# Transposing transfers that do not wait for one another: a fused state-space and feed-forward kernel

## The chip, the cores and the metric

The kernel runs on one core of a Trainium2 chip. The metric is the device time of one execution in microseconds (us). Before the change three runs took 178.19, 178.19 and 178.47 us, a median of 178.19. The core has engines that run at the same time, each with its own queue of instructions in a fixed order: TensorE (PE: matmuls; PEld: its weight loads), VectorE (DVE), ScalarE (ACT), GpSimd (POOL), and SyncE (SP), which here only issues transfers. They wait for one another through semaphores.

## The reference

The input x has 2048 rows of 512. It is normalized row by row, and the normalized xn feeds two branches whose results are added to x:

```
xn  = layernorm(x)
# A: a diagonal complex recurrence over the rows
Lam_bar = exp(dt * Lam);  B_bar = ((Lam_bar - 1) / Lam)[:, None] * B
h_t = Lam_bar * h_(t-1) + B_bar @ xn_t             (512 complex states)
A   = 2 * Re(C @ h_t) + xn * Dskip
# B: a gated feed-forward layer of width 1376
B   = (silu(xn @ w_gate) * (xn @ w_up)) @ w_down
out = x + A + B
```

All inputs and the output are bfloat16.

## The kernel before

The 2048 rows are cut into 4 chunks of 512, and each chunk into 4 tiles of 128 rows. Per chunk c the steps are: statistics and normalization of the four tiles (`bnst`, `bnag`, `ve`, `rstd`, `xn`); a transposition of the normalized tiles into xnT[c], with the features on the partitions; the gate and up matmuls (line 760), whose results ScalarE takes out of the accumulator banks (`silu` in line 772, `uev` in line 830) and VectorE multiplies into hT (line 832); the input matmuls of the recurrence against BT (line 881), which ScalarE takes out into u_sb (`uev_b`, line 888); the recurrence on VectorE, made real by rotating with cosine and sine tables, scanning (line 921) and rotating back into hss; and at last one accumulation of both branches into the output rows (lines 964, 978, 981), to which VectorE adds the residual (line 986) and which SyncE stores.

Chunk 0 is transposed on TensorE. Chunks 1 to 3 are transposed by a transposing transfer each, `xTd1` to `xTd3` (line 603), from xn_sb into xnT; for chunk 2 the destination lies in scrC, over the buffer tz that the tables use while they are made (`tm`, `tt1s`, `tzs`, `sinT`, `tt1c`, `tzc`, `cosT`, lines 707 to 722, once for each of 4 blocks). Four more transposing transfers bring in the weights of the recurrence: BT real and imaginary (`ld_bre`, `ld_bim`, lines 443 and 444) and C real and imaginary (`ld_cre`, `ld_cim`, lines 450 and 451). C lies in half of hss until ScalarE and VectorE have made W of it (lines 728 to 735).

All of these and nearly all plain loads go through SyncE's queue, in the order of the code: the x tiles of chunk 0 and the gate and up weights; the rows of chunk 1 (`ld_x4`); ld_bre, ld_bim, xTd1; the rows of chunks 2 and 3 (`ld_x8`, `ld_x12`) and Dskip (`ld_dsk`); ld_cre, ld_cim, xTd2; the down weights (`ld_wd0`, `ld_wd1`); xTd3; and the stores of the output.

Every transfer is made by the helper `dma` (line 394). A transposing one is given a dependence on all transfers created before it (line 397), and a plain one on the last transposing one (line 402). So a transposing transfer is never in flight together with any other transfer of the queue, and SyncE, which works in order, stands still in between.

The order on the engines is fixed when the program is built. `_schedule` is a planner: it gives each task a cost in ns and a priority (the longest path of costs behind it), keeps TensorE's and SyncE's tasks in the order of the code (`_CHAIN`), and fills the queues of VectorE, ScalarE and GpSimd by playing the program through. Of the tasks that could start within 200 ns of the earliest, it takes the one with the highest priority. A transfer counts as landed after 300 ns, its bytes at 330 bytes per ns behind the transfers ahead of it, and 2000 ns; a transposing one holds SyncE for 1900 ns and counts 1.2 times its bytes and 140,000 more, 769,145 for each of the seven. `_plan` then turns dependences into semaphore waits and leaves out those that an earlier wait already implies. `_emit` writes the instructions. The numbers of the planner decide the order alone; what the chip does is in the profile.

The accumulator has 8 banks, used as 4 pairs in rotation (`next_pair`, line 372). A pair is written by 8 matmuls, taken out by ScalarE, and written again four units later, so TensorE waits when ScalarE is more than three units behind.

Of the kernel before, what the change touches and what calls it, by code (L numbers as in the profile page):

```python
# [249 lines left out]
def bass_parallel_sum__ssm_conv_s5__swiglu_ffn__prompt_kernel(  # L250
# [32 lines left out]
    with es:  # L283
# [106 lines left out]

        dma_tasks = []
        xp_state = [None]

        def dma(name, dst, src, writes, nbytes, reads=(), after=(), out_=False, eng="sp", xpose=False, prio=0.0, order=(), **kw):
            after = tuple(after)
            if xpose:
                after = after + tuple(dma_tasks)
                fn = lambda e, dst=dst, src=src: e.dma_start_transpose(out=dst, in_=src)
                est, nb = 1900.0, int(nbytes * 1.2) + 140000
            else:  # L400
                if xp_state[0] is not None:
                    after = after + (xp_state[0],)
                fn = lambda e, dst=dst, src=src: e.dma_start(dst, src, **kw)
                est, nb = 330.0 + nbytes / 900.0, nbytes
            t = g.add(eng, fn, reads=reads, writes=writes, name=name, dma=True, after=after, out=out_, est=est, nbytes=nb, prio=prio, order=order)
            dma_tasks.append(t)
            if xpose:
                xp_state[0] = t
            return t

        TILEB = 128 * D * 2
# [4 lines left out]
        def pload(name, slot, src, **kw):  # L416
            return dma(name, prow[slot:128:8, :], src.rearrange("(a q j) -> q a j", a=4, q=4), [("prow", slot)], 1024, reads=[("prow0",)], **kw)

        def x_load(a, **kw):
            return dma("ld_x%d" % a, x_sb[:, a:a + 1, :], x_v[:, a:a + 1, :], [("x", a)], TILEB, **kw)  # L420

        def wg_load(nm, k0, k1, **kw):
            return dma("ld_wg" + nm, wg[:, k0:k1, 0:FG], wg_v[:, k0:k1, 0:FG], [("wg", nm)], (k1 - k0) * 128 * FG * 2, **kw)
# [659 lines left out]
```

## Time and profile before

The profiled execution took 178.43 us; its span from the first to the last instruction is 176.6 us.

| | |
|---|---|
| median of the runs | 178.19 us |
| profiled execution | 178.43 us |
| its span | 176.6 us |
| TensorE busy | 173.2 us, 98% |
| VectorE busy | 162.4 us, 92% |
| ScalarE busy | 87.1 us, 49% |
| GpSimd busy | 11.0 us, 6% |
| transposing transfers | 7, each 4.1 to 5.1 us from issue to landing |

How it is read: the page gives the busy time of each engine, then the span in 40 equal slices with the busy share of each in tenths (and the clock that TensorE was granted). The chain of work that ended last is followed back from the last instruction, and a list of it in order of time shows which engine set the pace when. A timeline lists the instructions of one engine, equal neighbours merged: start, duration, engine, line, operation, tile written and tiles read, count, and in square brackets how long the engine had been idle before and for whom. For SyncE the duration is that of the issue, not of the transfer. A list of waits says who waited for whom: total, times, longest.

### The profile page before, as it was taken

To read this page: it belongs to the slowest core of one execution; us is meant where nothing else is said; L and a number is where in the kernel's file an instruction comes from. 1 tells how busy PE (TensorE), PEld (TensorE's weight loads), DVE (VectorE), ACT (ScalarE), POOL (GpSimd) and SP (SyncE) were. 2 spreads that over 40 slices of the span, in tenths; PEclk is the share of its full clock that TensorE was granted. 3 is DMA by queue.
4 is the path that set the end of the run, shared out by engine and by line. 5 is a ranking of instruction groups with operands and counts; after the bars stand their busy time and mean duration, and the time that the engine had idled before them with its cause. 6 is when DMAs were issued, how large, how long until landed. Compare 5 with 4: busy or idle time off the path is not lost.

```text
span 176.6 us, 2364 instructions
## 1 busy us (share of the span) xinstructions
PE 173.2 (98%) x909; PEld 82.5 (47%) x916; DVE 162.4 (92%) x282; ACT 87.1 (49%) x116; POOL 11.0 (6%) x22
## 2 busy tenths in 40 slices
PE   8999999999999999999999999999999999999995
PEld 2894444444444444444444444444444444444543
DVE  2974999799999999999999999999999999999953
ACT  4679989979999668240456564000265620000000
POOL 3040500046000000000000000000000000000000
PEclk9999999999999999999999999999999999999999
DMA  5892668865675200001100000001100000000132
GB/s 169 269 370 75 119 137 103 267 121 119 119 267 132 43 0 0 0 4 60 61 0 0 0 0 4 0 0 59 59 0 4 0 0 0 0 0 4 41 119 78
DMA packets 22966, 12.37 MB, mean 70 GB/s; under 512 B 15308, under 2 KB 22956, under 8 KB 22956
## 3 DMA queue, kind: packets, MB, share of 16 engines
q1 hardware_dynamic: 22652, 11.77, 25.5%
q10 hardware_dynamic: 304, 0.46, 0.8%
q8 instruction: 7, 0.11, 0.3%
q14 instruction: 3, 0.02, 0.0%
HBM read 6.46 MB, written 2.10 MB: 48 GB/s over the span
## 4 chain that ended last, share of the span: by engine, by line
PE 96%; DMA 1%; DVE 1%; issue 0%; ACT 0%
PE pb L760 36%; PE pb L964 19%; PE pb L881 16%; PE pb L981 16%; PE pb L804 4%; PE pb L978 2%; PE pb L843 2%; DMA x_sb<-in_A_x_dram 1%; PE pb L853 1%; PE pb L583 1%; DVE st L529 0%; DVE xn_sb L516 0%; ACT sd L523 0%; DVE x_sb L986 0%; PE pb L476 0%
## 5 line engine op out<-in xcount | busy, mean ns | idle before, releaser
L921 DVE TENSOR_TENSOR_SCAN rot<-sm,car,rot 128x512 bf16<-128x512 f32 x32 | 38.7, 1265 | 0.0
L772 ACT ACTIVATE sg<-pb 128x1024 bf16<-128x1024 f32 x20 | 20.2, 1025 | 32.0 <-PE pb L760 31.3
L964 PE MATMUL pb<-wd,hT 128*128 128x512 bf16 (+2 forms) x166 | 34.7, 366 | 0.3 <-issue 0.2
L981 PE MATMUL pb<-W,hss 128*128 128x512 bf16 (+2 forms) x133 | 29.8, 366 | 0.2
L760 PE MATMUL pb<-xnT,wu 128*128 128x512 bf16 x120 | 27.9, 379 | 0.0
L964 PEld LDWEIGHTS pb<-wd,hT 128*128 128x128 bf16 x170 | 16.1, 98 | 18.9 <-ACT scrC L728 0.4
L830 ACT ACTIVATE uf<-pb 128x1024 bf16<-128x1024 f32 x20 | 20.5, 1026 | 7.6 <-PE pb L760 7.2
L760 PE MATMUL pb<-xnT,wg 128*128 128x512 bf16 x92 | 21.8, 379 | 0.0
L881 PE MATMUL pb<-xnT,BT 128*128 128x512 bf16 x96 | 21.2, 379 | 0.0
L981 PEld LDWEIGHTS pb<-W,hss 128*128 128x128 bf16 x136 | 12.9, 97 | 14.9
L888 ACT ACTIVATE u_sb<-pb 128x1024 bf16<-128x1024 f32 x16 | 16.3, 1020 | 5.3 <-PE pb L881 5.2
L760 PEld LDWEIGHTS pb<-xnT,wu 128*128 128x128 bf16 x120 | 11.7, 98 | 14.2 <-issue 0.2
L881 PEld LDWEIGHTS pb<-xnT,BT 128*128 128x128 bf16 x96 | 9.3, 98 | 11.6 <-DMA BT<-in_A_B_im_dram 0.5
L986 DVE TENSOR_TENSOR x_sb<-pb,x_sb 128x512 bf16<-128x512 f32 (+2 forms) x17 | 10.9, 655 | 3.5 <-PE pb L981 3.2
L760 PEld LDWEIGHTS pb<-xnT,wg 128*128 128x128 bf16 x92 | 9.0, 98 | 10.6
L832 DVE TENSOR_TENSOR hT<-sg,uf 128x1024 bf16<-128x1024 bf16 x20 | 13.4, 680 | 0.5 <-ACT uf L830 0.5
L481 DVE BATCH_NORM_STATS2 st<-x_sb 128x6 f32<-128x512 bf16 x12 | 7.5, 681 | 3.3 <-DMA x_sb<-in_A_x_dram 3.3
L912 DVE TENSOR_TENSOR rot<-u_sb,cosT 128x2048 bf16<-128x2048 bf16 x8 | 9.7, 1218 | 0.0
L912 DVE TENSOR_TENSOR rot<-rot,sin 128x2048 bf16<-128x2048 bf16 x8 | 9.7, 1218 | 0.0
L912 DVE TENSOR_TENSOR rot<-u_sb,sin 128x2048 bf16<-128x2048 bf16 x8 | 9.7, 1217 | 0.0
L912 DVE TENSOR_TENSOR rot<-rot,cosT 128x2048 bf16<-128x2048 bf16 x8 | 9.7, 1210 | 0.0
L912 DVE TENSOR_TENSOR rot<-rot 128x2048 bf16<-128x2048 bf16 x8 | 9.6, 1216 | 0.0
(93 smaller groups left out, 180.1 us busy)
## 6 DMA issues: line engine op xcount, KB each, us to landing
out_dram<-x_sb SPq DMA_DIRECT2D x15, 128.0 KB, 1.7
x_sb<-in_A_x_dram SPq DMA_DIRECT2D x3, 512.0 KB, 4.4
wd<-in_B_w_down_dram SPq DMA_DIRECT2D x1, 1280.0 KB, 6.2
wu<-in_B_w_up_dram SPq DMA_DIRECT2D x1, 768.0 KB, 5.0
wu<-in_B_w_up_dram SPq DMA_DIRECT2D x1, 608.0 KB, 7.1
x_sb<-in_A_x_dram SPq DMA_DIRECT2D x4, 128.0 KB, 3.4
wg<-in_B_w_gate_dram SPq DMA_DIRECT2D x1, 480.0 KB, 5.9
wg<-in_B_w_gate_dram ACTq DMA_DIRECT2D x1, 448.0 KB, 3.8
```

Of the source, the lines that this page charges most:

```text
L481: return g.add("dve", lambda e, a=a: e.bn_stats(out=st[:, a % 8, :], in_=x_sb[:, a, :]), reads=[("x", a)], writes=[("st", a % 8), ("st0", ...
L760: inst = e.matmul(pbank[0:fs, bk, :].rearrange("p (j t) -> p j t", j=4), lhsT=w[:, kt, i * 128:i * 128 + fs], rhs=xnT[c][:, :, kt, :], sta ...
L772: g.add("act", lambda e: e.activation(out=sg[rows, sl, 0:n, :].rearrange("p a t -> p (a t)"), in_=pair_f32(rows, bk, 512 * n), func=AF.Sil ...
L830: g.add("act", lambda e: e.activation(out=uf[rows, ul, 0:n, :].rearrange("p a t -> p (a t)"), in_=pair_f32(rows, bk, 512 * n), func=AF.Ide ...
L832: g.add("dve", lambda e: e.tensor_tensor(out=hT[rows, hb, i0:i0 + n, :], in0=sg[rows, sl, 0:n, :], in1=uf[rows, ul, 0:n, :], op=ALU.mult), ...
L881: inst = e.matmul(pbank[:, bk, :].rearrange("p (j t) -> p j t", j=4), lhsT=BT[:, ri, kt, pt * 128:(pt + 1) * 128], rhs=xnT[c][:, :, kt, :] ...
L888: g.add("act", lambda e: e.activation(out=u_sb[:, us].rearrange("p r t -> p (r t)"), in_=pair_f32(slice(0, 128), b0), func=AF.Identity), r ...
L912: tt = lambda out, a, b, op, r, w, nm: g.add("dve", lambda e: e.tensor_tensor(out=out, in0=a, in1=b, op=op), reads=r, writes=w, name="%s_% ...
L921: g.add("dve", lambda e, A0=A0, A1=A1, k=k, ri=ri, pt=pt: e.tensor_tensor_scan(out=A1[:, k, ri, :], data0=rr[:, pt:pt + 1].to_broadcast([1 ...
L964: inst = e.matmul(pbank[:, bk, 0:nc_], lhsT=hT[0:fs, hb, i, lt * 128:(lt + 1) * 128], rhs=wd[0:fs, i, c0:c0 + nc_], start=(i == 0), stop=F ...
L981: inst = e.matmul(pbank[:, bk, 0:nc_], lhsT=hss[:, hb, pt, ri, lt * 128:(lt + 1) * 128], rhs=W12[:, ri, pt, c0:c0 + nc_], start=False, sto ...
L986: g.add("dve", lambda e, bk=bk, a=a, c0=c0, nc_=nc_: e.tensor_tensor(out=x_sb[:, a, c0:c0 + nc_], in0=pbank[:, bk, 0:nc_], in1=x_sb[:, a, ...
```

## The change

A transposing transfer is no longer given a dependence on the transposing transfers ahead of it, only on the plain ones. A new list keeps the transposing ones, so that they can be left out. Dependences through data stay (a transposition of xn_sb still waits for the normalized tiles, and one into scrC for the readers of tz). A plain transfer depends on the last transposing one as before. The seven transposing transfers form the groups {ld_bre, ld_bim, xTd1}, {ld_cre, ld_cim, xTd2} and {xTd3}; within a group none waits any more for the landing of another. The planner sees the new dependences too.

```diff
         dma_tasks = []
         xp_state = [None]
+        xp_tasks = []
 
         def dma(name, dst, src, writes, nbytes, reads=(), after=(), out_=False, eng="sp", xpose=False, prio=0.0, order=(), **kw):
             after = tuple(after)
             if xpose:
-                after = after + tuple(dma_tasks)
+                after = after + tuple(t for t in dma_tasks if t not in xp_tasks)
                 fn = lambda e, dst=dst, src=src: e.dma_start_transpose(out=dst, in_=src)
                 est, nb = 1900.0, int(nbytes * 1.2) + 140000
...
             dma_tasks.append(t)
             if xpose:
                 xp_state[0] = t
+                xp_tasks.append(t)
             return t
```

## The prediction

> **What bounds the kernel now.** I read the engine totals and slices first, then the chain in order of time, then SyncE's queue and its waits, and last VectorE and ScalarE between 29 and 43 us, where the change reaches them.
>
> Totals and slices of the page:
>
> ```profile
> PE 173.2 (98%) x909; PEld 82.5 (47%) x916; DVE 162.4 (92%) x282; ACT 87.1 (49%) x116; POOL 11.0 (6%) x22
> PE   8999999999999999999999999999999999999995
> PEclk9999999999999999999999999999999999999999
> ```
>
> TensorE is busy from the second slice to the last, at the full granted clock; VectorE is close behind. The chain in order of time (start, length):
>
> ```profile
> 24.06 0.86 PE pb L881 x4
> 24.93 0.01 issue
> 24.93 13.12 PE pb L881 x60
> 38.06 17.27 PE pb L760 x80
> ```
>
> From 4.96 us on the chain is TensorE alone up to 174.82, with no piece of another engine between. 80 matmuls in 17.27 us are 0.216 us each, and no longer stretch runs slower. The order of TensorE's matmuls is that of the code, so the end can come earlier only where TensorE stands still. The pieces called issue after 5.4 us sum to 0.52 us; most lie where one matmul record is missing from a row (x39 for 40, x7 for 8). The one piece that touches a transfer of this change is 0.01 us, at 24.93, for BT's imaginary half.
>
> SyncE's queue (start, duration of the issue), and two of its waits:
>
> ```profile
> 16.25 2.26 SPq L398 DMA_TRANSPOSE BT<-in_A_B_re_dram  x1
> 20.74 1.99 SPq L398 DMA_TRANSPOSE BT<-in_A_B_im_dram  x1
> 24.96 2.93 SPq L398 DMA_TRANSPOSE xnT<-xn_sb  x1
> 30.07 0.93 SPq L403 DMA_DIRECT2D x_sb<-in_A_x_dram  x2
> ...
> 35.28 1.85 SPq L398 DMA_TRANSPOSE hss<-in_A_C_re_dram  x1
> ```
> ```profile
> SPq L398 <- DMA BT<-in_A_B_re_dram: 2.2, 1, 2.2
> SPq L244 <- DMA BT<-in_A_B_im_dram: 2.2, 1, 2.2
> ```
>
> Each transposing transfer takes 1.7 to 2.9 us to issue, and the next waits 2.2 to 2.5 us more for the landing. Four such waits go: 2.2 + 2.2 here, 2.5 + 2.4 at the two halves of C (the second is issued at 39.68, xTd2 behind it at 43.89).
>
> VectorE and ScalarE around the statistics of chunk 2:
>
> ```profile
> 29.94 1.29 DVE L711 SCALAR_TENSOR_TENSOR scrC<-scrC 128x512 f32<-128x512 f32 x2
> 31.14 0.76 DVE L717 TENSOR_SCALAR scrC<-scrC 128x512 f32<-128x512 f32 x2
> 31.81 0.68 DVE L719 SCALAR_TENSOR_TENSOR scrC<-scrC 128x512 f32<-128x512 f32 x1
> 33.44 2.47 DVE L481 BATCH_NORM_STATS2 st<-x_sb 128x6 f32<-128x512 bf16 x4 [0.94 <-DMA x_sb<-in_A_x_dram]
> ...
> 36.11 0.66 DVE L719 SCALAR_TENSOR_TENSOR scrC<-scrC 128x512 f32<-128x512 f32 x1
> ```
> ```profile
> 36.80 0.72 ACT L721 ACTIVATE cosT<-scrC,halfpi 128x512 bf16<-128x512 f32 x1 [1.04 <-DVE scrC L719]
> ...
> 38.71 2.93 ACT L505 ACTIVATE xn_sb<-x_sb,nmr,rstd 128x512 bf16<-128x512 bf16 x4 [0.28 <-DVE nmr L502]
> 41.55 1.01 ACT L888 ACTIVATE u_sb<-pb 128x1024 bf16<-128x1024 f32 x1
> ```
>
> VectorE waited 0.94 us for the rows of chunk 2, and ScalarE ran the four normalizations of chunk 2 ahead of one eviction that TensorE needs. That is TensorE's thinnest margin here: the eviction at 41.55 ends at 42.56, and its pair of banks is wanted 24 matmuls after 38.06, at 43.24.
>
> **The first group: BT real, BT imaginary, xTd1, the rows of chunk 2.** The real half stays at 16.25, since it waits for the plain load of chunk 1. The imaginary half can be issued at 16.25 + 2.26 = 18.5 instead of 20.74 and lands about 2.2 us earlier. On the path that is worth the 0.01 us; TensorE's weight loads lose a wait of 0.5 us there, hidden under matmuls, so 0.01 to 0.5 bounds the gain and I take 0.01, the matmuls' own row. xTd1 cannot move as far as its two waits suggest: it needs the four normalized tiles, whose row ends at 22.91, so it goes from 24.96 to about 22.95, a gain of 2.0. TensorE wants it at 24.06 + 32 x 0.216 = 30.97 and had it at about 30.05, so this gains nothing on the path; the cover is the 32 matmuls of chunk 0. xTd1 took 5.1 us to land; the other two transfers of its kind took 4.2 and 4.3. I take 5.1, the same transfer at nearly the same place: landing at 28.1, with 27.2 as the other end. The rows of chunk 2 took 30.07 to 33.44 = 3.37 us until VectorE read them, so they arrive at L = 31.5 (ends 30.6 and 31.5).
>
> **The order that the planner writes.** The landing estimates are inputs of the order on VectorE and ScalarE. By the planner's own arithmetic for before (its numbers decide order only; no time is taken from them) the rows of chunk 2 land at 31.7. With the imaginary half issued at 15.7 and landing at 20.7, xTd1 waits for the tiles at 20.9 and lands at 25.5, and the rows at 29.5. VectorE is free there at 29.6, after tzs2; bnst8 has priority 144.8 against 143.5 for tzs3. So the four statistics should move ahead of tzs3, tt1c2, tt1c3 and tzc2. Nothing ahead of that point changes place: the priorities of chunk 1's statistics fall by some 9 us but stay the highest.
>
> Cost of that, with durations of the trace: tzs2 ends at 30.6, VectorE then waits until L = 31.5, 0.9 us against 0.94 before. Statistics to the next instruction are 33.44 to 36.11 = 2.67, so tzs3 starts at L + 2.67 and its reader on ScalarE, sinT3, at L + 3.39 (the same pair at 23.43 and 24.15 shows 0.72). Behind sinT3 in ScalarE's queue I work out this order: one eviction (uev_b1_1), cosT2, the four normalizations, cosT3, then uev_b1_2. With starts 0.54, 0.90, 0.61, 2.84 and 0.61 apart (24.15 to 24.69, 42.45 to 43.35, 32.73 to 33.34, 38.71 to 41.55, and 0.61 again) uev_b1_2 starts at L + 8.89 and ends 1.01 later, L + 9.90, and some 0.06 passes to TensorE: L + 9.96 = 41.46. TensorE wants those banks 16 matmuls after 38.06, at 41.51. The stall is max(0, L - 31.55), so zero at the value taken, with 0.05 in hand; at L = 30.6 there is 0.95. The eviction after it, uev_b1_3, ends about 0.9 later, 42.4, against 43.24. ScalarE's other work up to there has room.
>
> **The second group: C real, C imaginary, xTd2, xTd3.** C real starts where the plain loads have landed, 2 us earlier; C imaginary follows it without 2.5. xTd2 then waits no longer for C but for cosT3, which reads the buffer it overwrites: about L + 8.28 + 0.72 = 40.5, plus the queue, so 41 against 43.89. That stall moves rather than goes. Nothing was waiting: xTd2 landed at 48.1 and is read from 55.16; wd landed at 54.6 and is read at 67.69; xTd3 landed near 58.9 and is read near 64.8; C landed by 43.9 and ScalarE first reads it at 51.60, in an order set by priority. Bounds: no gain above 0, no loss while covers of 4 us and more stand. W and the last gate tile (hL) have the thinnest later cover: hL ends at 74.08 against 76.11, 2.0 us; VectorE's wait at L would have to grow by that.
>
> Waits added: a reader of both C halves waits on two semaphores in place of one, on ScalarE at 51 us, off the path. Instructions, bytes and matmuls are the same.
>
> [...] All seven transposes are rows of SPq. [...]
>
> **Sum.** 0.01 gained, 0.00 lost. The profiled execution took 178.43 us (span 176.6 and 1.83 around it), 0.24 above the median of 178.19; the sum gives 178.42 on its own scale and 178.2 on the median's.
>
> **Rivals.**
>
> Stall behind the new order (slower): L comes later than 31.55, because xTd1 or the rows land slower than before. For it: the margin worked out is 0.05 us. Against: 5.1 was already the slowest of three. The end is later by L - 31.55; from L = 31.92 it exceeds 0.2%. At 32.4 it is 179.0.
>
> The halves of BT share the engines and land together (slower): nothing shows two in flight. The real half has 24.06 - 20.74 = 3.3 us in hand, so this decides only if it lands after 24.06. If both came only when the second came before, at 24.85, TensorE would stand 0.8 us: 179.0. Against: the second is issued 2.3 us behind the first, which should be half through.
>
> A gain at BT's imaginary half (faster): in unprofiled runs that wait might be larger than 0.01. The most the rows allow is the 0.5 of the weight loads: 177.7.
>
> The change does not do what it says: the second issue stays blocked until the first has landed and its row becomes 4 us long. Then all is as before, 178.2.
>
> **How the numbers follow.** 0.2% is 0.36 us, about what this kernel's measurement can tell from no change. Likeliest, no stall: 0.66, 178.2. No effect in the queue: 0.05, 178.2. Stall behind the new order beyond 0.36 us: 0.15. Halves together: 0.06. Gain beyond 0.36 us: 0.08. So faster 0.08, same 0.71, slower 0.21. The range goes from 177.95, half the bound of 0.5 below, to 179.0, where both slower rivals have their worked-out values; about 1 in 10 is left out.
>
> **What would show it.** Right: in SyncE's queue the imaginary half at 18.5 and xTd1 near 23; the statistics of chunk 2 directly behind one L711; the four normalizations near 36.9, ahead of the last cosT; TensorE's chain unbroken past 41.5. Wrong: a TensorE gap at 41.5 ended by ScalarE's L888, or at 24.06 ended by BT's real half, or a gap later ended by VectorE. A gain above 0.4 us would mean that TensorE waits in unprofiled runs where this profile shows none.

## The result, and the profile after

The changed kernel takes 179.22 us (median of 22 runs), the kernel before took 178.44 in the runs beside it: a ratio of 1.0046, with an interval of 1.0032 to 1.0060. The change makes the kernel 0.46% slower. The forecast was 178.2 us, no change, with a range up to 179.0; the second likeliest case, a stall behind the new order, was given 0.15, and it is what happens, but more often and larger than it was priced. A quarter of a microsecond of the miss is scale: the forecast stood on three runs of before with a median of 178.19, and 22 runs have 178.44. A ratio with its interval is given as recorded; it is not the quotient of the two medians beside it, and differs from that by up to 0.11%.

The runs of the changed kernel spread from 178.27 to 180.33 us, those of before from 178.10 to 179.02. They fall into two groups: with the 12 further runs of e1, 9 of 34 lie at 178.20 to 178.78 and 25 at 179.11 to 180.33, and none lies between. The profiled execution of the changed kernel took 178.51 us, less than nearly all its runs; its profile shows the new order but not the typical loss. A later profiled execution of the same kernel (run e11) took 179.88 us. Both are shown. Line numbers after the change are 1 or 2 higher.

Totals and slices of the page of the changed kernel (178.51 us):

```profile
PE 173.6 (98%) x909; PEld 83.0 (47%) x916; DVE 162.9 (92%) x282; ACT 87.9 (50%) x116; POOL 11.3 (6%) x22
PE   8999999999999999999999999999999999999995
```

Its chain in order of time (start, length), without a break where the BT matmuls and the gate and up matmuls of chunk 1 are:

```profile
24.33 13.81 PE pb L883 x64
38.14 17.27 PE pb L762 x80
55.41 6.91 PE pb L883 x32
```

Its queue of SyncE (start, duration of the issue):

```profile
15.95 2.08 SPq L399 DMA_TRANSPOSE BT<-in_A_B_re_dram  x1
18.09 3.24 SPq L399 DMA_TRANSPOSE BT<-in_A_B_im_dram  x1
22.72 1.77 SPq L399 DMA_TRANSPOSE xnT<-xn_sb  x1
27.30 0.93 SPq L404 DMA_DIRECT2D x_sb<-in_A_x_dram  x2
...
32.59 1.85 SPq L399 DMA_TRANSPOSE hss<-in_A_C_re_dram  x1
34.48 2.83 SPq L399 DMA_TRANSPOSE hss<-in_A_C_im_dram  x1
39.86 1.70 SPq L399 DMA_TRANSPOSE scrC<-xn_sb  x1
```

The waits are gone: each second transfer is issued as soon as the first issue is over, xTd1 is issued when the normalized tiles are there, and what follows is 2 to 5 us earlier. VectorE and ScalarE of the same execution:

```profile
29.70 0.68 DVE L713 SCALAR_TENSOR_TENSOR scrC<-scrC 128x512 f32<-128x512 f32 x1
30.65 2.47 DVE L483 BATCH_NORM_STATS2 st<-x_sb 128x6 f32<-128x512 bf16 x4 [0.27 <-DMA x_sb<-in_A_x_dram]
33.04 0.36 DVE L487 BATCH_NORM_AGGREGATE mv<-st 128x2 f32<-128x6 f32 x4
33.32 0.66 DVE L713 SCALAR_TENSOR_TENSOR scrC<-scrC 128x512 f32<-128x512 f32 x1
```
```profile
35.65 0.71 ACT L723 ACTIVATE cosT<-scrC,halfpi 128x512 bf16<-128x512 f32 x1
36.26 2.92 ACT L507 ACTIVATE xn_sb<-x_sb,nmr,rstd 128x512 bf16<-128x512 bf16 x4
39.08 0.71 ACT L723 ACTIVATE cosT<-scrC,halfpi 128x512 bf16<-128x512 f32 x1
39.69 1.91 ACT L890 ACTIVATE u_sb<-pb 128x1024 bf16<-128x1024 f32 x2
```

The statistics of chunk 2 now stand between the two L713, and on ScalarE the four normalizations and the last cosT stand ahead of two evictions. Here the rows came at 30.65 and nothing was late. In the execution of 179.88 us they came at 32.89. Its queue of SyncE, its VectorE, its ScalarE and its TensorE:

```profile
23.27 1.76 SPq L399 DMA_TRANSPOSE xnT<-xn_sb  x1
29.29 0.93 SPq L404 DMA_DIRECT2D x_sb<-in_A_x_dram  x2
```
```profile
32.89 2.48 DVE L483 BATCH_NORM_STATS2 st<-x_sb 128x6 f32<-128x512 bf16 x4 [1.95 <-DMA x_sb<-in_A_x_dram]
```
```profile
38.30 2.92 ACT L507 ACTIVATE xn_sb<-x_sb,nmr,rstd 128x512 bf16<-128x512 bf16 x4
...
41.74 1.91 ACT L890 ACTIVATE u_sb<-pb 128x1024 bf16<-128x1024 f32 x2
```
```profile
39.70 1.89 PE L762 MATMUL pb<-xnT,wu 128*128 128x512 bf16 x8
42.80 1.90 PE L762 MATMUL pb<-xnT,wg 128*128 128x512 bf16 x8 [1.20 <-ACT u_sb L890]
```

xTd1 took 6.02 us from issue to landing instead of the 4.58 of the first profile, VectorE waited 1.95 us for the rows, the eviction began at 41.74, and TensorE stood still for 1.20 us. That time is never made up: in the chain of that execution TensorE is without a piece of another engine from 42.80 to 176.28 us, 2 us before the end.

### The profile page after: what moved, and what is told of

The parts are those of the page before. It is cut to its first block, busy times and chain, and to the rows that moved or that the text cites. A ratio compares the mean times of both kernels' runs of the same rounds, so it can differ in the third digit from the quotient of the medians.

```text
span 176.7 us, 2363 instructions
## 1 busy us (share of the span) xinstructions
PE 173.6 (98%) x909; PEld 83.0 (47%) x916; DVE 162.9 (92%) x282; ACT 87.9 (50%) x116; POOL 11.3 (6%) x22
## 4 chain that ended last, share of the span: by engine, by line
PE 98%; issue 0%; DVE 0%
PE pb L762 36%; PE pb L966 19%; PE pb L883 16%; PE pb L983 16%; PE pb L806 4%; PE pb L478 3%; PE pb L980 2%; PE pb L845 2%; PE pb L855 1%; PE pb L585 1%; DVE x_sb L988 0%
## 5 line engine op out<-in xcount | busy, mean ns | idle before, releaser
L890 ACT ACTIVATE u_sb<-pb 128x1024 bf16<-128x1024 f32 x16 | 16.2, 1020 | 5.6 <-PE pb L883 5.4
L762 PE MATMUL pb<-scrC,wu 128*128 128x512 bf16 x40 | 9.4, 379 | 0.0
```

The costliest lines, as they stand in the source:

```text
L762: inst = e.matmul(pbank[0:fs, bk, :].rearrange("p (j t) -> p j t", j=4), lhsT=w[:, kt, i * 128:i * 128 + fs], rhs=xnT[c][:, :, kt, :], sta ...
L890: g.add("act", lambda e: e.activation(out=u_sb[:, us].rearrange("p r t -> p (r t)"), in_=pair_f32(slice(0, 128), b0), func=AF.Identity), r ...
```

## The experiments

The change does two things at once: it changes the waits on the chip, and, through the planner, the order on VectorE and ScalarE. The experiments take them apart. The changed kernel again (e1), the order alone (e2), the waits alone (e3) and a partial version (e4) ran on one chip, beside 29 runs of before with a median of 178.68 us.

**e1: the changed kernel again.**

> The changed kernel once more, for another profiled execution: the one at hand took 178.51 us, faster than nearly all its other runs (median 179.22), so it may not show what makes the typical run slow. Every theory expects a ratio near 1.005. Stall behind the new order: where the profiled execution is a slow one, TensorE stands still at about 41.6 us for ScalarE's eviction, and VectorE has waited longer than 0.3 us for the rows of chunk 2. Transfers in flight together: a gap at 24 to 31 us, ended by BT or by xTd1. Slow start: TensorE reaches its full rate later than 4.2 us, and the whole loss lies before 13 us.

Measured: 179.23 us, as at first; the ratio is 1.0020 (1.0001 to 1.0039). The profiled execution took 179.74: VectorE began the statistics at 32.74, and TensorE has a gap of 1.03 us that ends at 42.65 with ScalarE's eviction (L890). There is no gap at 24 to 31 us.

**e2: the new order with the old waits.**

```diff
+                xp_before[name] = tuple(xp_tasks)
                 after = after + tuple(t for t in dma_tasks if t not in xp_tasks)
...
         streams = _schedule(g.tasks, engs)
+        for t in xp_tasks:
+            t.deps.update(xp_before[t.name])
```

> The planner sees the new dependences, so the order on VectorE, ScalarE and GpSimd is that of the changed kernel, but the waits between the transposing transfers are put back after planning. The rows of chunk 2 then reach VectorE at about 33.4 us as before the change. Stall behind the new order: a stall of 33.4 - 31.55 = 1.9 us at TensorE near 41.5, ratio 1.010. Transfers in flight together: no pair is in flight, so ratio 1.000. Slow start from GpSimd's changed first instructions: ratio 1.005.

Measured: 180.38 us, ratio 1.0094 (1.0075 to 1.0112). The order alone costs 1.7 us. TensorE of this kernel:

```profile
25.22 13.12 PE L885 MATMUL pb<-xnT,BT 128*128 128x512 bf16 x60 [0.30 <-DMA BT<-in_A_B_im_dram]
...
43.73 1.90 PE L764 MATMUL pb<-xnT,wg 128*128 128x512 bf16 x8 [1.94 <-ACT u_sb L892]
```

The gap of 1.94 is the one that the theory of the order expected at 1.9; that the size fits so well is in part luck, since the rows came at 33.83 and not at 33.4, and TensorE was itself 0.46 us late by BT's imaginary half. No two transposing transfers were in flight together here, so that cannot be the cause.

**e3: the new waits with the old order.**

```diff
-                after = after + tuple(t for t in dma_tasks if t not in xp_tasks)
+                after = after + tuple(dma_tasks)
...
         streams = _schedule(g.tasks, engs)
+        for t in xp_tasks:
+            t.deps.difference_update(xp_tasks)
```

> The planner sees the old dependences, so the order on every engine is that of before, and the waits between the transposing transfers are taken out after planning. Stall behind the new order: nothing is late, ratio 1.000 (0.998 to 1.002). Transfers in flight together: ratio 1.005 as in the changed kernel, with a gap at 24 to 31 us. Slow start: 1.000.

Measured: 178.29 us, ratio 0.9976 (0.9961 to 0.9990): faster than before, where the theory of the order expected no change. Taking the waits out is a small gain; planning with them out is the loss.

**e4: only the BT group freed.**

```diff
-                after = after + tuple(t for t in dma_tasks if t not in xp_tasks)
+                after = after + tuple(t for t in dma_tasks if t not in xp_tasks or name not in ("ld_bre", "ld_bim", "xTd1"))
```

> Only the group BT real, BT imaginary, xTd1 is freed; C real, C imaginary and xTd2 wait as before. The order on VectorE and ScalarE is that of the changed kernel, GpSimd's first instructions are in the order of before. Stall behind the new order: ratio 1.005, as the changed kernel. Transfers in flight together at BT: 1.005; if the C group does the harm, 1.000. Slow start from GpSimd's order: 1.000.

Measured: 179.13 us, ratio 1.0019 (1.0005 to 1.0032), the same as the changed kernel beside it. The order on VectorE and ScalarE is the same too; the C group is not needed for the loss, and GpSimd's first instructions, which are back in the old order here, are not its cause. In the profiled execution, of 178.51 us, the rows came at 30.89 and there is no gap.

**e5 and e6: which wait is the gain.** Beside 29 runs of before with a median of 178.62 us. In e5, a version of the kernel before, the order stays and one wait goes:

```diff
         streams = _schedule(g.tasks, engs)
+        xp = {t.name: t for t in g.tasks if t.name in ("ld_bre", "ld_bim")}
+        xp["ld_bim"].deps.discard(xp["ld_bre"])
+        [t for t in g.tasks if t.name == "xTd1"][0].deps.add(xp["ld_bre"])
```

> Order on every engine as before; only the wait of BT's imaginary half for the landing of the real half is taken out (xTd1 still waits for both, the C group as before). If the gain of the waits alone (ratio 0.9976) is TensorE's wait for the imaginary half at 24.9 us, which lands on the edge in the kernel before, this shows all of it: 0.9976 (0.996 to 0.999). If the gain comes from earlier rows of chunk 2 or from the C group, 1.000.

In e6 only the C group is freed, which leaves the order on VectorE, ScalarE and GpSimd as it was:

```diff
-                after = after + tuple(t for t in dma_tasks if t not in xp_tasks)
+                after = after + tuple(t for t in dma_tasks if t not in xp_tasks or name not in ("ld_cre", "ld_cim", "xTd2"))
```

> Order as before on every engine, only C real, C imaginary and xTd2 are freed of one another. Nobody waited for them on the path: 1.000 (0.998 to 1.002) by every theory but one that puts the gain of the waits alone into this group, which expects 0.9976.

Measured: e5 178.28 us, ratio 0.9983 (0.9974 to 0.9992); e6 178.81, ratio 1.0002 (0.9986 to 1.0018). The gain comes with the wait between the two halves of BT. In e5 xTd1 and the rows of chunk 2 also come earlier, so e5 alone does not exclude these; the sum over all executions, below, leaves nothing for them.

**e8 and e14: before, again.**

> The kernel before once more, for another profiled execution. Its runs spread from 178.18 to 179.67, wider than those of the waits alone (178.14 to 178.77). If the spread is TensorE's wait for BT's imaginary half, an execution above 178.5 us shows a gap of that size at 24.9 us, ended by that transfer; if it is the start, the gap is before 13 us.

> The kernel before a third time. A gap at about 25 us ended by BT's imaginary half, of 0 to 0.8 us, the later the landing the longer. Start: 12.5 to 12.75 if a late start belongs to the changed order, as likely 12.9 if it is chance.

These executions took 179.01 and 178.71 us. TensorE of the first and of the second:

```profile
25.52 13.12 PE L881 MATMUL pb<-xnT,BT 128*128 128x512 bf16 x60 [0.73 <-DMA BT<-in_A_B_im_dram]
```
```profile
25.19 13.12 PE L881 MATMUL pb<-xnT,BT 128*128 128x512 bf16 x60 [0.34 <-DMA BT<-in_A_B_im_dram]
```

The kernel before has a gap of 0 to 0.7 us at BT's imaginary half; in the profile on which the prediction was made it was 0.01. With the old waits this gap was 0.01, 0.73, 0.34, 0.30 (e2), 0.51 (e6) and 0 (e12), 0.32 on average. No execution with the wait taken out has it.

The time lost is 0.16 us more than such a gap. A 128x512 matmul is 0.38 us long in the trace, but without a wait the next one begins 0.216 us behind its start; a gap is counted from the end of the matmul ahead. Even the first profile shows the loss, in the length of its 64 BT matmuls against those of e3:

```profile
23.90 14.16 PE L881 MATMUL pb<-xnT,BT 128*128 128x512 bf16 x64
```
```profile
23.81 13.98 PE L883 MATMUL pb<-xnT,BT 128*128 128x512 bf16 x64
```

From the first BT matmul to the next gate tile it is 13.81 to 13.82 us where nothing waits, and 0.17 us more in the first profile, 0.89 in e8, 0.50 in e14, 0.68 in e6, 0.46 in e2 and nothing in e12: 0.45 on average. The medians of e3, e5 and e10 lie 0.29 to 0.39 us under those of before, which is the same size.

**e7: one eviction moved in the changed kernel.**

```diff
         streams = _schedule(g.tasks, engs)
+        act = streams["act"]
+        u = [t for t in act if t.name == "uev_b1_2"][0]
+        act.remove(u)
+        act.insert([t.name for t in act].index("xn8"), u)
```

> The changed kernel, with one task moved after planning: the eviction uev_b1_2 stands ahead of the four normalizations of chunk 2 in ScalarE's queue instead of behind cosT3. Stall behind the new order: TensorE's pair of banks is out about 3.4 us earlier, no gap at 41.5, and the time is that of the waits alone, ratio 0.9976 (0.996 to 0.999), not 1.002 to 1.005. The next eviction, uev_b1_3, still stands behind the normalizations and would end at about L + 10.0, wanted near 43.3, so rows as late as L = 33.2 cost nothing. Any other cause of the loss (transfers in flight together, a slow start): it stays at 1.002 to 1.005.

Measured: 178.53 us, ratio 1.0000 (0.9990 to 1.0010). ScalarE and TensorE:

```profile
36.45 1.02 ACT L890 ACTIVATE u_sb<-pb 128x1024 bf16<-128x1024 f32 x1
37.37 2.92 ACT L507 ACTIVATE xn_sb<-x_sb,nmr,rstd 128x512 bf16<-128x512 bf16 x4
```
```profile
39.70 1.89 PE L762 MATMUL pb<-xnT,wu 128*128 128x512 bf16 x8
41.43 1.89 PE L762 MATMUL pb<-xnT,wg 128*128 128x512 bf16 x8
```

With the eviction ahead of the normalizations the gap is gone, and 0.7 us of the changed kernel's time with it (179.23 in e1, on another chip). But the kernel is not as fast as e3, as was expected; it is 0.24 us slower, and the expectation failed by that.

**e9 to e15: what is left.** e7 and e3 again on one chip, and single profiled executions for the start and the gap.

> The kernel of e7 once more, for its start. In e7 TensorE had no gap at 41.5 and yet took 0.25 us more than the waits alone; in the profiles all of that lies before 13 us, where TensorE reached its full rate at about 5.9 us instead of 3.4 to 5.5 in the kernels with the order of before. If that start is chance, this median falls to 178.3 and the profiled start may be early; if it belongs to this program, the median stays near 178.5 and the profiled start is late again.

> The kernel of e3 once more, beside e9 on the same chip. The waits alone were 0.9976 of before: expected again 0.9970 to 0.9990, and a profile without a gap at 24.9 or 41.5. If the start is chance, its profiled start may be as late as in e7.

> The changed kernel a third time, for one profiled execution. Stall behind the new order: with L the time at which VectorE begins the statistics of chunk 2, TensorE's gap near 41.5 is L + 9.9 less the time at which it wants the banks (41.5 to 41.65), within 0.2 us, and nothing if that is below zero.

> The kernel of e2 once more, for one profiled execution. Gap near 41.5 of L + 9.9 less the time at which TensorE wants the banks, as in e2 (1.94). Start: if the late start belongs to the changed order, the first 128x512 matmuls begin at 12.9 or later; if it is chance, as likely at 12.5 to 12.75 (e2 itself began at 12.67).

> The kernel of e7 a third time. No gap at 41.5. Start: 12.9 or later if it belongs to the changed order, as likely 12.5 to 12.75 if it is chance.

> The kernel of e5 once more. No gap at 25 us and none at 41.5. Start: 12.5 to 12.75 if a late start belongs to the changed order, as likely 12.9 if it is chance.

Measured: e9 178.68 us, ratio 1.0003 (0.9990 to 1.0016); e10 178.31 us, ratio 0.9974 (0.9959 to 0.9988); the single ones e11 179.88, e12 179.99, e13 178.25, e15 178.19 us. The gap, over all profiled executions that have the changed order on ScalarE with no eviction moved (the time lost is what lies between the starts of the two rows around the gap, less the usual 1.73 us):

| | statistics of chunk 2 begin (L) | matmuls after the gap begin | L + | gap, us | lost, us |
|---|---|---|---|---|---|
| changed | 30.65 | | | 0 | 0 |
| e4 | 30.89 | | | 0 | 0 |
| e1, changed | 32.74 | 42.65 | 9.91 | 1.03 | 1.19 |
| e11, changed | 32.89 | 42.80 | 9.91 | 1.20 | 1.37 |
| e12, old waits | 33.01 | 42.91 | 9.90 | 1.61 | 1.77 |
| e2, old waits | 33.83 | 43.73 | 9.90 | 1.94 | 2.09 |

Where there is a gap, it ends 9.90 to 9.91 us after the statistics begin, whatever the waits were.

Three numbers of a trace account for its whole time: the start of the first 128x512 matmuls (gate tile 7), the time lost at BT's imaginary half, and the time lost at the banks near 41.5 us. What is left of the profiled time is 165.56 to 165.63 us in all 17 profiled executions, of every version. Some of them, in us:

| | start | lost at BT | lost at the banks | profiled time | the rest |
|---|---|---|---|---|---|
| before | 12.68 | 0.17 | 0 | 178.43 | 165.58 |
| e8, before | 12.54 | 0.89 | 0 | 179.01 | 165.58 |
| changed | 12.94 | 0 | 0 | 178.51 | 165.57 |
| e11, changed | 12.94 | 0 | 1.37 | 179.88 | 165.57 |
| e2, order alone | 12.67 | 0.46 | 2.09 | 180.85 | 165.63 |
| e3, waits alone | 12.59 | 0 | 0 | 178.16 | 165.57 |
| e7, eviction moved | 12.94 | 0 | 0 | 178.50 | 165.56 |

So in these executions nothing else in the change costs or brings time.

The 0.24 us of e7 and the 0.37 of e9 over the waits alone lie at the start, as far as the profiles show it: e7 and e9 were profiled at 178.50 and 178.64 us and begin at 12.94 and 13.04, e3 and e10 at 178.16 and 178.31 and begin at 12.59 and 12.75. TensorE's first 128x512 matmuls begin 0.43 us apart, the later ones at the full rate, 0.216. By the starts of single matmuls, the full rate came between 3.4 and 5.8 us with the order of before (at 4.5 us in the first profile), and later than 6.1 us in the six late executions (at 6.3 us in the first profile of the changed kernel). It varies from execution to execution of the same program: e7 began at 12.94 us, and e13, its program again, at 12.65 and took 178.25 us, as fast as e3. What sets the moment was not shown. The clock row of the pages does not show it: it reads full from the first slice on, though the record behind it begins only at 4.28 us in the first profile and at 6.24 in the first of the changed kernel, and eight of the 17 pages have no such row.

Late starts were 6 of 9 executions with the changed order and 0 of 8 with the order of before. If each execution drew its start by itself, all six would fall among these nine about once in 150 times, and e9 (178.68 us) beside e10 (178.31), 12 runs each on one chip, is what the expectation of e9 gave for a start that belongs to the program. But e2, e12 and e13 have the changed order and an early start. What in the program brings the late start stays open: the order of the instructions ahead of 13 us differs only in GpSimd's first few, and e4, which has these in the old order, started late as well.

The fastest versions are e3 and e5. e3 beat the kernel before in both sets of runs (0.9976, interval 0.9961 to 0.9990, and 0.9974, interval 0.9959 to 0.9988) and the changed kernel by 0.9 us.

## Why the prediction was wrong

The new order was right to the instruction: the statistics ahead of tzs3, and on ScalarE one eviction, cosT2, four normalizations, cosT3, uev_b1_2. So was the cost chain: L + 9.96 was worked out, 9.90 measured. So was the place, 41.5 us, and the threshold: 31.55 was worked out, and e11 has 31.52 (the row would have begun at 39.70 + 1.73 = 41.43, less 9.91). That the threshold agrees to 0.03 us is partly luck, since TensorE began 0.26 us later in e11 than in the profile that was read.

**The step that failed is the term "I take 5.1" for the landing of xTd1, and L = 31.5 from it.** In the executions in which the wait between the halves of BT is out xTd1 landed after 4.57 (e4), 4.58, 4.66 (e9), 4.68 (e7) or after 5.59 (e5), 5.66 (e3), 5.93 (e1), 6.01 (e10, e15) and 6.02 us (e11, e13): never near the 5.1 that it takes with the old waits (5.03 to 5.24 in six executions). The two bounds of the prediction, 4.2 and 5.1, did not hold the upper group, and L went to 32.9, not 31.5. In e11, 0.92 us of that is the landing (6.02 for 5.1), 0.32 the issue of xTd1 (23.27 for 22.95; the statistics of chunk 1 had already begun 0.34 us later than before), and 0.23 the rows (3.60 for 3.37; they took 3.33 to 3.66 in the other executions that waited for them). Each of the three is more than the 0.05 us in hand. So zero stall was not the likeliest case: 25 of the 34 runs of the changed kernel lie in the slower group, and the profiled executions above 179 us lost 1.19 and 1.37 us at the banks. This moves most of the 0.66 to the rival that was given 0.15. "The same transfer at nearly the same place" was the reason for 5.1, and it does not hold: the last section shows what the transfer meets when it comes 2 us earlier.

**The wait at BT's imaginary half** was taken at 0.01 us, from the one profiled execution, with 0.5 as the other end. The gap is 0.32 us on average over six executions and reached 0.73, and the time lost is 0.45 on average and reached 0.89; even the execution that was read lost 0.17. So this gain was real, and it hides part of the stall: the rival "a gain at BT's imaginary half" held at the same time as the stall. What is lost or gained at different places adds up; the prediction treated the rivals as alternatives.

**Halves of BT that land together** did not happen on the path: no execution with the waits out shows a gap at 24 us. **The second group** cost and brought nothing that e6 could show (1.0002, 0.9986 to 1.0018), as worked out. The stall at xTd2 moved to cosT3, as said, and was hidden. The start, at 12.92 to 13.04 us in most executions with the changed order and at 12.54 to 12.75 with the order of before, was not in the sum at all.

On the median's scale: the changed kernel is 0.9 us above e3 and e10, which have its waits. 0.54 to 0.7 of that is the gap (e9 and e7 against the changed kernel), and 0.24 to 0.37 what the profiles put at the start. Against before, some 0.3 us is gained at BT.

## What to carry to other kernels

A dependence that a planner sees is two changes in one: a wait on the chip and an input of the order of everything else. When taking a wait out, keep the order of before and take it out of the emitted waits alone, then try the new order by itself; here the waits alone are 0.24% faster than before and the order alone is 0.94% slower. Where a margin is 0.05 us and hangs on a transfer, one profiled execution shows one draw of its landing, and a wait of 0.01 us in it may be 0.3 on average.

## What the runs showed of the hardware that was not expected

xTd1, the same 512 KB from SBUF to SBUF, took 5.03 to 5.24 us with the old waits and either 4.57 to 4.68 or 5.59 to 6.02 us without. It is not that it was in flight with another transposing transfer: in e5 and e15 it waited for both halves of BT and took 5.59 and 6.01. In e1 its bytes moved until about 27.2 us, and the landing was seen at 29.2. In the windows of half a microsecond of e1 the bytes moved fall as follows (GB/s, from the stretches' DMA column, which counts a packet where it begins): 26.0 to 26.5, 216; 26.5 to 27.0, 175; 27.0 to 27.5, 42; 27.5 to 28.0, 0; up to 30.0, nothing.

The single DMA packets of the kept traces show what lies in between. Every execution has one packet of 16 KB of the queue that the pages call "q8 instruction" that begins between 25.5 and 27.3 us and lasts 0.92 to 1.40 us. There are three cases:

- It comes directly behind xTd1's last packet (changed, e4, e7, e9). xTd1's data move for 2.7 to 2.8 us, and it landed after 4.57 to 4.68.
- It comes between xTd1's last data and its last two packets of 4 bytes (e1, e10, e11, e13, e15). The data again move for 2.7 to 2.8 us, but the two packets wait: in e1 the instruction packet lasts from 27.17 to 28.10, they end at 28.11, 15 of the 16 signals of the landing are there by 27.63 and the last at 29.18. xTd1 landed after 5.93 to 6.02.
- It lies alongside xTd1's data, which then move for 3.4 to 3.9 us (e3 and e5, and all six with the old waits). xTd1 landed after 5.59 to 5.66 in the first two, and after 5.03 to 5.24 with the old waits, the 5.1 of the prediction among them.

So the 5.1 already held the cost of this packet, and the transfer moved 2 us earlier meets it at another place. The other two transfers of its kind, with 4.2 and 4.3 us before the change, have no such packet among their data. That both use the same one of the 16 DMA engines is inferred, from packets that follow each other without a break; the traces kept here do not name the engine. Why the packet comes ahead of the last 4 bytes in one execution and behind them in another stays open.

The halves of BT, issued one behind the other with no wait, took 2.0 to 3.2 us to issue, where with the wait they took 1.8 to 2.4. The real half landed after 4.6 to 5.5 us (4.2 to 4.6 with the wait), the imaginary half after 4.4 to 5.3 (4.1 to 4.6). In these runs two in flight in one queue did not block each other, but the first of them mostly took longer.
